# Attention and gated expert in one kernel: later chunks' output products with high and low parts side by side, first outputs in float32, and four weight tiles' low parts formed on TensorE

## The chip, the cores and the metric

The kernel runs on one core of a Trainium2 chip. The metric is the device time of one execution in microseconds (us), taken as the median of repeated runs; a shorter time is better.

## The reference

The first half is a gated recurrence per batch and head (4 batches, 8 heads, 768 steps, head dimension 48); the second is an RMS norm and a gated expert over the 3072 tokens of width 384, with a hidden width of 1536.

```
for t in range(S):
    state = alpha[:, :, t, :, None] * state + np.einsum('bhd,bhe->bhde', k[:, :, t], v[:, :, t])
    y[:, :, t] = np.einsum('bhd,bhde->bhe', q[:, :, t], state)
...
rms = np.sqrt(np.mean(x * x, axis=-1, keepdims=True) + 1e-06)
xn = x / rms * rms_g
g = xn @ w_gate
silu = g * (1.0 / (1.0 + np.exp(-g)))
val = xn @ w_val
return (silu * val @ w_out).astype(np.float32)
```

All inputs and outputs are float32; the weights reach the kernel as 64-bit words from which it takes float32.

## The kernel before

**Numbers in two parts.** Nearly every matmul operand is split in a high and a low float16 part: ScalarE (ACT) rounds to the high part, VectorE (DVE) subtracts it from the float32 value and rounds the rest to the low part. A product of two such operands is the sum of three float16 products, high by high, high by low and low by high (`SPLIT = ((0, 0), (0, 1), (1, 0))`, line 29).

**Attention.** The sequence is cut in 24 chunks of 128 tokens (`attention(cc, due)`); chunk cc belongs to batch cc mod 4, so chunks 0 to 3 are the first of their batches. For one chunk two scans of `alpha` (L549), products with k and q (L564, L569), and their low parts (L576, L603) come from DVE. Scores (`scores`, L639; in float32 for the first four chunks, L647) go to PSUM buffers with the tag `at`, of which there are three. DVE multiplies them by the mask (L652), ACT rounds to the high part (L663), DVE forms the low part (L666, `a_lo`, called `al` in the plan). `output` (L670) then makes the chunk's output `y`, 128 tokens by 8 heads of 48 columns, from two kinds of products: state by query (L680, 48 rows of weights, not for the first four chunks) and scores by v (L689, 128 rows of weights). For each of the four pairs of heads and each half j of a pair there are three products of either kind, 48 columns wide. `y` has one PSUM buffer of two banks (tag `y`, `y=1` in `BUFS`). From it ACT takes the sum of squares (L738), DVE multiplies by the RMS gain (L758); after a root on GpSimd (L754) the rows are scaled and split into `x16` (L762, L765) and transposed by a DMA into `xT` (L776). `sums` (L706) makes the state's update.

**Weights.** Eighteen tiles (`decode`): for each, ACT folds the exponent (L485), DVE does three integer steps (L494, L497, L502), ACT writes the high part (L452) and DVE the low part (L510, `wl` in the plan). Tiles i0 to i11 hold `w_gate` and `w_val`, o0 to o5 `w_out`.

**Expert.** Chunks are taken in groups of 4, 2, 2, 4, 4, 4 and 4. For each group and each of twelve blocks f of the hidden width, `expert_in` makes gate and value (L877), ACT takes silu (L888), DVE the product (L894, "gate" below), ACT and DVE its two parts (L452, L907); `expert_out` multiplies by `w_out` (L934), DVE scales the sums (L945) and a DMA stores them. In group 0 the blocks f = 0 to 2 are done in halves: first chunks 0 and 1, then 2 and 3.

**Order.** All this is entered in a `Plan` with an engine, a cost, dependences, buffers and due times. `Plan.order` (L91) walks through it once and fixes a static order for every engine; each engine then works through its own list in that order. A changed cost or operation can so move instructions all over the program.

Of the kernel before, what the change touches and what calls it, by code (L numbers as in the profile page):

```python
# [44 lines left out]
EARLY = 3  # L45

BUFS = dict(
# [8 lines left out]
    abs=0.92, wh=0.83, pow=0.65, sc=0.8, sc32=2.3, y=0.87, y0=0.5, u=0.45, po=1.48,  # L56
)
IN_COST = {4: (1.95, 0.49, 0.6, 0.63), 2: (0.99, 0.28, 0.34, 0.4)}
# [8 lines left out]
STRIDE = [0, 8, 12, 12, 20, 20, 20]  # L67


class Plan:  # L70
# [9 lines left out]
    def op(self, engine, cost, fn, deps=(), use=(), due=None, lock=False, kb=0):  # L80

        o = dict(e=engine, c=cost, fn=fn, d=[d for d in deps if d], u=tuple(use), due=due, lock=lock,
                 kb=kb, i=len(self.ops), n=[])
# [7 lines left out]
    def order(self):  # L91
        for o in reversed(self.ops):
            lat = WAIT.get(o["e"], LOAD_LAG + LOAD_END + 1.5)
            due = [n["s"] - lat for n in o["n"]] + ([o["due"]] if o["due"] is not None else [])
            o["s"] = min(due, default=1e6) - o["c"]
        free = {t: [(0.0, i) for i in range(n)] for t, n in BUFS.items()}
# [218 lines left out]
def tile_attn_moe(  # L315
# [97 lines left out]
    mask = const.tile([P, 2, 1, C], F32, name="mask")  # L413
    eps = const.tile([P, 1], F32, name="eps")
    rare = const.tile([P, 1], F32, name="rare")
    for h, rows in enumerate((slice(HC, P), slice(0, HC))):
        a0 = S_A[1] / (S_K[h] * S_Q[1])
        nc.gpsimd.memset(mask[rows, 0], a0)
        nc.gpsimd.memset(mask[rows, 1], a0 * S_QP)
    nc.gpsimd.affine_select(  # L420
        mask,
        mask,
        pattern=[[0, 2], [0, 1], [1, C]],
# [4 lines left out]
    )  # L428
    for h, rows in enumerate((slice(0, HC), slice(HC, P))):
# [7 lines left out]
    NH = len(GROUPS) * NF + EARLY  # L437
# [25 lines left out]
    def add(engine, kind, *args, **kw):  # L463
        return op(engine, COST[kind], *args, **kw)

    def decode(src, dst, name, col):
# [44 lines left out]

        raw, wu = ("raw", name), ("wu", name)
        o = op("SP", 0.9, load, [], [raw], kb=786)
# [3 lines left out]
        o = add("DVE", "rest", rest, [o], [raw, wu], lock=True)  # L517
        o = add("ACT", "wh", high, [o], [wu])
# [9 lines left out]
    def attention(cc, due):  # L528
# [129 lines left out]

        def a_tile():
# [76 lines left out]

        def square():
            nc.scalar.activation(  # L738
                like(junk), t["y"][:, :, :HW], AF.Square, accum_out=ssq[:, cc : cc + 1]
            )  # L740
# [15 lines left out]
        def gain():  # L756
            t["x32"] = tl(ap, [P, DM], F32, "x32")
            nc.vector.tensor_tensor(like(t["x32"]), t["y"][:, :, :HW], like(rg), op=ALU.mult)  # L758
# [55 lines left out]
        m0 = add("DVE", "mask", lambda: masked(0), [sc], [at0])  # L814
        m1 = add("DVE", "mask", lambda: masked(1), [sc], [at1])
        a0 = add("ACT", "a16", lambda: a_hi(0), [m0], [at0, key("a16")])
        a1 = add("ACT", "a16", lambda: a_hi(1), [m1], [at1, key("a16")])
# [363 lines left out]
```

## Time and profile before

| | |
|---|---|
| median of 3 runs | 570.16 us (568.27, 570.16, 570.45) |
| the profiled execution | 569.0 us, of which its span 567.0 us |
| TensorE (PE) busy | 513.2 us, 91% of the span |
| VectorE (DVE) busy | 411.5 us, 73% |
| ScalarE (ACT) busy | 239.0 us, 42% |

The span runs from the first to the last instruction on the core, and 2.0 us lie around it. Times in the trace count from the start of the span. Matmuls overlap each other, so that the mean length of one matmul is more than its share of the engine's time; what one costs is read from when the next begins.

### The profile page before, as it was taken

Reading aid. Unit: us, or ns where it says so; the run is one execution under the profiler, and the core shown is the slowest. Engines: PE = TensorE matmul, PEld = TensorE weight load, DVE = VectorE, ACT = ScalarE, POOL = GpSimd, SP = SyncE. Lnnn points to the kernel's source line nnn. Section 1 sums busy time; section 2 is a strip of 40 time slices with the busy share of each in tenths; the row PEclk is TensorE's granted clock in tenths of the full one; section 3 lists DMA queues with packets and bytes.
Section 4 is the critical chain, followed back from the end, with each engine's and each line's share of the span. In section 5 each row is a group of like instructions: output and inputs, shape, how many; then the busy total and the mean of one; then the engine's idle time right before and its main releaser. Section 6 shows DMA issues by size and latency. Waiting matters only on the chain.

```text
span 567.0 us, 12116 instructions
## 1 busy us (share of the span) xinstructions
PE 513.2 (91%) x4994; PEld 299.3 (53%) x4994; DVE 411.5 (73%) x739; ACT 239.0 (42%) x640; POOL 18.9 (3%) x47
## 2 busy tenths in 40 slices
PE   2445998697899899999999999999999999999995
PEld 1434643254686678644456644456545456544462
DVE  7999899999998799967877678775377643133303
ACT  2555666544444476244452245452255531133300
POOL 1100000000000000000000010000000000000000
PEclk9998899898999999999999999999999999999999
DMA  8994345567640773342334235232211101000001
GB/s 213 308 286 116 117 163 181 181 194 192 167 132 16 150 161 89 100 112 45 80 97 85 88 105 105 32 88 73 71 30 18 15 15 45 28 1 0 1 29 34
DMA packets 59695, 56.15 MB, mean 99 GB/s; under 512 B 39472, under 2 KB 54960, under 8 KB 57168
## 3 DMA queue, kind: packets, MB, share of 16 engines
q1 hardware_dynamic: 59632, 55.30, 37.6%
q8 instruction: 41, 0.67, 0.5%
q14 instruction: 22, 0.18, 0.1%
HBM read 41.26 MB, written 4.72 MB: 81 GB/s over the span
## 4 chain that ended last, share of the span: by engine, by line
PE 74%; DVE 11%; issue 1%; DMA 1%; ACT 1%; ACTq 0%
PE mm L877 41%; PE mm_po L934 22%; PE y L689 4%; PE at L639 2%; PE y L680 2%; PE at L706 1%; DVE h L907 1%; DVE h L894 1%; DVE wu_i L497 1%; DVE wu_o L502 1%; DVE wg L510 1%; DVE wu_o L497 1%; DVE wu_i L502 1%; DVE at L652 1%; DMA kT<-k 1%
## 5 line engine op out<-in xcount | busy, mean ns | idle before, releaser
L877 PE MATMUL mm<-xT,wg 128*128 128x512 f16 (+1 forms) x1566 | 292.8, 346 | 9.8 <-ACT wg L452 5.5
L877 PEld LDWEIGHTS <-wg 128*128 128x128 f16 x1566 | 151.9, 99 | 136.3 <-ACT wg L452 7.1
L934 PE MATMUL mm_po<-wo,h 128*128 128x384 f16 x864 | 149.9, 332 | 7.5 <-DVE wo L510 3.9
L934 PEld LDWEIGHTS <-h 128*128 128x128 f16 x864 | 84.2, 99 | 66.3 <-issue 14.2
L452 ACT ACTIVATE h<-h 128x512 f16<-128x512 f32 (+1 forms) x87 | 48.1, 553 | 83.6 <-DVE h L894 83.4
L894 DVE SCALAR_TENSOR_TENSOR h<-mm,sl 128x512 f32<-128x512 f32 (+1 forms) x87 | 51.7, 594 | 42.0 <-PE mm L877 42.0
L907 DVE TENSOR_TENSOR h<-h,h 128x512 f16<-128x512 f32 (+1 forms) x87 | 51.3, 591 | 20.1 <-ACT h L452 20.0
L888 ACT ACTIVATE sl<-mm 128x512 f32<-128x512 f32 (+1 forms) x87 | 45.1, 518 | 46.7 <-PE mm L877 46.1
L549 DVE TENSOR_TENSOR_SCAN att<-att,seed 112x520 f32<-112x520 f32 x48 | 59.2, 1236 | 5.3 <-DMA att<-att 4.9
L945 DVE TENSOR_SCALAR ob<-mm_po 128x384 f32<-128x384 f32 x24 | 13.2, 553 | 34.6 <-PE mm_po L934 34.6
L663 ACT CAST a<-at 128x512 f16<-128x512 f32 x48 | 28.0, 585 | 23.5 <-DVE at L652 23.3
L652 DVE TENSOR_TENSOR at<-at,mask 128x512 f32<-128x512 f32 x48 | 31.2, 693 | 5.1 <-PE at L639 4.9
L666 DVE TENSOR_TENSOR a<-at,a 128x512 f16<-128x512 f32 x48 | 30.9, 683 | 0.4
L689 PE MATMUL y<-v,a 128*128 128x48 f16 x576 | 30.4, 190 | 0.0
L647 PE MATMUL at<-qp,kh 48*128 48x128 f32 x64 | 10.4, 443 | 21.1 <-DVE qp L569 15.9
L754 POOL TENSOR_TENSOR ss<-ss,mhalf 128x1 f32<-128x1 f32 x24 | 15.7, 655 | 379.9 <-DVE ss L744 361.2
L738 ACT ACTIVATE junk<-y 128x384 bf16<-128x384 f32 x24 | 11.8, 492 | 28.0 <-DVE x L758 14.1
L689 PEld LDWEIGHTS <-a 128*128 128x128 f16 x576 | 21.3, 100 | 3.9 <-issue 0.7
L452 ACT ACTIVATE v<-v 128x384 f16<-128x384 f32 x24 | 12.5, 520 | 25.2 <-PE at L706 25.2
L576 DVE TENSOR_TENSOR k<-kh,k 112x512 f16<-112x512 f32 x24 | 16.5, 689 | 8.8 <-ACT k L452 8.7
L452 ACT ACTIVATE k<-kh 112x512 f16<-112x512 f32 x24 | 15.0, 625 | 18.4 <-DMA kT<-k 9.3
L758 DVE TENSOR_TENSOR x<-y,rg 128x384 f32<-128x384 f32 x24 | 13.3, 553 | 11.7 <-PE y L689 8.4
(86 smaller groups left out, 391.5 us busy)
## 6 DMA issues: line engine op xcount, KB each, us to landing
att<-att SPq DMA_DIRECT2D x22, 903.0 KB, 5.6
v<-vtok SPq DMA_DIRECT2D x24, 192.0 KB, 3.1
raw_i<-w_gate SPq DMA_DIRECT2D x12, 384.0 KB, 3.3
raw_i<-w_val SPq DMA_DIRECT2D x12, 384.0 KB, 4.0
raw_o<-w_out SPq DMA_DIRECT2D x6, 768.0 KB, 4.4
out_dram<-ob SPq DMA_DIRECT2D x24, 192.0 KB, 2.1
att<-att SPq DMA_DIRECT2D x4, 227.5 KB, 3.8
att<-att SPq DMA_DIRECT2D x2, 448.0 KB, 7.6
```

The costliest lines, as they stand in the source:

```text
L452: nc.scalar.activation(dst, src, AF.Copy, scale=scale, accum_out=stat[:rows, col : col + 1])
L549: nc.vector.tensor_tensor_scan(x, x, start.rearrange("r g p c -> r (g p c)"), 0.0, op0=ALU.mult, op1=ALU.add)
L576: nc.vector.tensor_tensor(t["k16"][:, 1], t["kh"], t["k16"][:, 0], op=ALU.subtract)
L652: nc.vector.tensor_tensor(t["sc"][j], t["sc"][j], mask[:, int(first)].to_broadcast([P, NP, C]), op=ALU.mult,)
L663: nc.scalar.copy(a_tile()[:, j, 0], t["sc"][j])
L666: nc.vector.tensor_tensor(a_tile()[:, j, 1], t["sc"][j], a_tile()[:, j, 0], op=ALU.subtract)
L689: nc.tensor.matmul(yps[:, j, cs], a_tile()[:, j, x, p, :], t["v16"][:, y, j, p, :], start=first and m == 0, stop=m == 2,)
L877: nc.tensor.matmul(ps[:, :n], wg[:, f, x, j, kk, :], xT[:, y, kk, cs], start=i == 0, stop=i == 3 * NK - 1,)
L888: nc.scalar.activation(t["sl"][:, :n], t[0][:, :n], AF.Silu, scale=1.0 / (S_X * S_W))
L894: nc.vector.scalar_tensor_tensor(t["h"][:, :n], t[1][:, :n], S_H / (S_X * S_W), t["sl"][:, :n], op0=ALU.mult, op1=ALU.mult,)
L907: nc.vector.tensor_tensor(h16_of(g, f)[:, 1, cs], t["h"][:, :n], h16_of(g, f)[:, 0, cs], op=ALU.subtract)
L934: nc.tensor.matmul(t[i][:, :DM], h16_of(g, f)[:, x, ts], wo[:, f // 2, y, f % 2, :], start=f == 0 and m == 0, stop=f == NF - 1 and m == 2,)
```

## The change

1. **Wide outputs.** For chunks 10 to 23 (`WIDE`), the high part of the weights is multiplied with both parts of the other operand at once, 96 columns wide, and the low part with the high part alone, 48 columns wide. A pair of heads then takes 8 products instead of 12. The results stand in two columns of sums in PSUM; ACT copies one of them to `x32` (`take`), DVE adds the other (`add_up`), and the sum of squares and the gain read `x32` in place of PSUM.
2. **First outputs in float32.** For chunks 0 to 3 (`OUT32`) the mask is multiplied straight into a float32 tile in the place of `a16`, and eight float32 products by the unsplit v give `y`. The rounding (L663) and the low part (L666) are dropped for them.
3. **Four low parts by TensorE.** For weight tiles i0 to i3 (`LOW_W`), TensorE multiplies the float32 tile by an identity into the `y` buffer, then adds minus the high part; ACT writes the rest as the low part. DVE's L510 is dropped for them.
4. **Constants** for this (a third mask, an identity in float32 and its negative in float16) are made by GpSimd at the start. Other new names (`LATE`, `LOW_A`, `LOW_H`, `CUTS`, `SIDE`, more costs) leave the plan as it was with the values given: `LOW_A` and `LOW_H` are empty.

```diff
+OUT32 = 4
+WIDE = range(10, 24)
+LOW_A = ()
+LOW_H = ()
+LOW_W = ("i0", "i1", "i2", "i3")
...
+        def bring():
+            t["ps"] = buf(ps_y, [P, 2, 512], F32, "y", name)
+            for n in range(2):
+                nc.tensor.matmul(
+                    t["ps"][:, n, : NW // 2], same, t["uf"][:, n * (NW // 2) : (n + 1) * (NW // 2)],
+                    start=True, stop=False,
+                )
+
+        def less():
+            for n in range(2):
+                nc.tensor.matmul(
+                    t["ps"][:, n, : NW // 2], minus, dst[:, 0, n * (NW // 2) : (n + 1) * (NW // 2)],
+                    start=False, stop=True,
+                )
+
+        def residue():
+            nc.scalar.copy(
+                dst[:, 1].rearrange("p (n c) -> p n c", n=2), t["ps"][:, :, : NW // 2]
+            )
...
+        if name in LOW_W:
+            ps = ("y", name)
+            o0 = add("PE", "wid", bring, [o], [wu, ps])
+            o = add("ACT", "wh", high, [o], [wu])
+            o = add("PE", "wneg", less, [o, o0], [ps])
+            return add("ACT", "wl2", residue, [o], [ps])
...
+            nc.vector.tensor_tensor(
+                tile_of(("a16", cc), make)[:, j],
+                t["sc"][j],
+                mask[:, 2].to_broadcast([P, NP, C]),
+                op=ALU.mult,
+            )
...
+                    nc.tensor.matmul(
+                        t["y"][:, j, p * D : (p + 1) * D],
+                        tiles["a16", cc][:, j, p, :],
+                        v[:, j, p, :],
+                        start=True,
+                        stop=True,
+                    )
...
+        def output_wide(h):
+            if h == 0:
+                t["y"] = tl(ps_y, [P, 2, 512], F32, "y")
+            for p in (2 * h, 2 * h + 1):
+                at = [t["y"][:, j, 2 * p * D : 2 * (p + 1) * D] for j in range(2)]
+                for x in range(2):
+                    for j in range(2):
+                        r = slice(64 * j, 64 * j + D)
+                        nc.tensor.matmul(
+                            at[j][:, : (2 - x) * D],
+                            t["q16"][r, x, p, :],
+                            states[b][2][r, : 2 - x, p, :],
+                            start=x == 0,
+                            stop=False,
+                        )
+                for j in range(2):
+                    for x in range(2):
+                        nc.tensor.matmul(
+                            at[j][:, : (2 - x) * D],
+                            a_tile()[:, j, x, p, :],
+                            t["v16"][:, : 2 - x, j, p, :],
+                            start=False,
+                            stop=x == 1,
+                        )
...
+            nc.scalar.copy(t["ys4"], y_part(1))
...
+            nc.vector.tensor_tensor(t["ys4"], y_part(0), t["ys4"], op=ALU.add)
...
+        if cc < OUT32:
+            m0 = add("DVE", "mask", lambda: masked32(0), [sc], [at0, key("a16")])
+            m1 = add("DVE", "mask", lambda: masked32(1), [sc], [at1, key("a16")])
+            ins = [key("a16"), key("v"), key("y")]
+            y0 = add("PE", "y32", lambda: output32(0), [m0, m1, lv], ins)
+            y1 = add("PE", "y32", lambda: output32(1), [y0], ins)
...
+        if cc in WIDE:
+            y_k = key("x32")
+            y1 = add("ACT", "take", take, [y1], [key("y"), y_k])
+            y1 = add("DVE", "add", add_up, [y1], [key("y"), y_k])
+        sq = add("ACT", "sq", square, [y1], [y_k])
+        x = add("DVE", "x", gain, [sq if cc in WIDE else y1, tiles["rg"]], [y_k, key("x32")], lock=cc in WIDE)
```

**VectorE around the first gate of the expert** (`h32_0_0_0`, chunks 0 and 1, f = 0), before: the last chunk of group 0 and the scans of chunk 4 stand ahead of it (`att`, `qp`, `x16`: the number behind is the chunk's; L549 is a scan).

```order
L765 SCALAR_TENSOR_TENSOR x16_2_529<-x32_2_457,ss_2_455,x16_2_529 128x384
L549 SCALAR_TENSOR_TENSOR att_4_178<-att_4_178,seed_91 112x520
L744 TENSOR_SCALAR ss_3_547<-ssq_115,eps_98 128x1
L758 TENSOR_TENSOR x32_3_549<-y_3_511,rg_90 128x384
...
L549 SCALAR_TENSOR_TENSOR att_4_178<-att_4_178,seed2_95 112x520
L765 SCALAR_TENSOR_TENSOR x16_3_566<-x32_3_549,ss_3_547,x16_3_566 128x384
L894 SCALAR_TENSOR_TENSOR h32_0_0_0_591<-mm_0_0_0_1_568,sl_0_0_0_578 128x256
```

The same place now (L602 is a scan, L898 the low part of x, L1046 the gate; `wu_i3` is the fourth weight tile).

```order
L602 SCALAR_TENSOR_TENSOR att_5_233<-att_5_233,seed2_95 112x520
L622 TENSOR_TENSOR qp_5_468<-att_5_233 112x2x4x64
L656 SCALAR_TENSOR_TENSOR q16_4_451<-qp_4_398,q16_4_451 112x512
...
L529 SCALAR_TENSOR_TENSOR wu_i3_512<-raw_i3_297,wu_i3_512 128x768
L891 TENSOR_TENSOR x32_3_532<-y_3_490,rg_90 128x384
...
L602 SCALAR_TENSOR_TENSOR att_6_383<-att_6_383,seed_91 112x520
L898 SCALAR_TENSOR_TENSOR x16_3_551<-x32_3_532,ss_3_525,x16_3_551 128x384
L1046 SCALAR_TENSOR_TENSOR h32_0_0_0_571<-mm_0_0_0_1_554,sl_0_0_0_564 128x256
```

Scans of chunks 5 and 6, query products of chunks 4 and 5 and the integer steps of tiles i2 and i3 have moved ahead of the first gate, which is VectorE's instruction 81 now and was 71.

**TensorE at the first outputs**, before: the output of chunk 0 is 24 float16 products between the float32 scores of chunks 1 and 2 (`y_0`, `at_1`, `at_2`).

```order
L647 MATMUL at_1_1_198<-qp_1_174,kh_1_170 128x128
L689 LDWEIGHTS a16_0_185
L689 MATMUL y_0_212<-v16_0_189,a16_0_185 128x48
...
L647 MATMUL at_2_0_255<-qp_2_247,kh_2_225 128x128
L647 MATMUL at_2_1_256<-qp_2_247,kh_2_225 128x128
```

Now (`x8` and `x2`: so many float32 products alike; `y_i0` is the weight tile i0 in the `y` buffer).

```order
L700 MATMUL at_1_1_199<-qp_1_186,kh_1_182 128x128
L732 MATMUL y_0_214<-v_0_145,a16_0_193 128x48 x8
L700 MATMUL at_2_0_237<-qp_2_230,kh_2_228 128x128
...
L700 MATMUL at_2_1_238<-qp_2_230,kh_2_228 128x128
L732 MATMUL y_1_257<-v_1_147,a16_1_221 128x48 x8
L542 MATMUL y_i0_292<-wu_i0_235,same_109 128x384 x2
L549 LDWEIGHTS minus_107
L549 MATMUL y_i0_292<-wg_130,minus_107 128x384
```

The buffer `y` is now used in the order y_0, y_1, i0, i1, y_2, y_3, i2, i3, and the first product of the expert stands behind y_3, as before.

**TensorE in an output of a later chunk**, before: the end of the six state products of a pair, and the first of its six products of scores by v (chunk 12).

```order
L680 LDWEIGHTS q16_12_3144
L680 MATMUL y_12_3589<-s160_375,q16_12_3144 128x48
L689 LDWEIGHTS a16_12_3571
L689 MATMUL y_12_3589<-v16_12_3484,a16_12_3571 128x48
L689 LDWEIGHTS a16_12_3571
```

Now, the last three of a pair's four state products and the first two of its four products by v.

```order
L748 MATMUL y_12_3498<-s160_367,q16_12_3079 128x96
L748 LDWEIGHTS q16_12_3079
L748 MATMUL y_12_3498<-s160_367,q16_12_3079 128x48
...
L757 LDWEIGHTS a16_12_3481
L757 MATMUL y_12_3498<-v16_12_3391,a16_12_3481 128x96
L757 LDWEIGHTS a16_12_3481
L757 MATMUL y_12_3498<-v16_12_3391,a16_12_3481 128x48
```

A chunk has 32 products instead of 48, half of them 96 columns wide.

## Rows read from the trace of the kernel before

**Rows 1.** The page: span, and each engine's busy time, share and instructions.

```profile
span 567.0 us, 12116 instructions
PE 513.2 (91%) x4994; PEld 299.3 (53%) x4994; DVE 411.5 (73%) x739; ACT 239.0 (42%) x640; POOL 18.9 (3%) x47
```

**Rows 2.** Stretches: start:end, length, busy us of each engine, PEclk (TensorE's granted clock).

```profile
0.00:42.80 42.80, 16.64 (x257) 14.36 (x258) 38.17 (x62) 18.86 (x49) 4.42 (x21) 1.00 1.01 270
42.80:55.20 12.40, 6.52 (x43) 4.49 (x39) 12.29 (x21) 6.86 (x22) 0.55 (x1) 0.93 0.33 84
55.20:132.10 76.90, 65.88 (x395) 34.23 (x396) 74.06 (x109) 44.53 (x114) 0.72 (x5) 0.92 0.55 170
132.10:150.50 18.40, 15.95 (x246) 10.12 (x246) 17.30 (x36) 7.20 (x18) 1.10 (x2) 0.91 0.63 164
150.50:196.20 45.70, 44.07 (x625) 34.41 (x625) 40.80 (x85) 20.89 (x69) 1.41 (x2) 1.00 0.48 116
196.20:474.90 278.70, 278.05 (x2991) 157.88 (x2984) 203.79 (x382) 123.23 (x330) 10.12 (x15) 1.00 0.32 73
```

**Rows 3.** Chain that ended last, 129 to 198: start, us, what.

```profile
131.20 0.87 DVE wo L510
...
143.65 2.93 PE mm_po L934 x18
...
149.28 0.61 DVE a L666
...
150.49 22.70 PE mm L877 x207
```

**Rows 4.** TensorE's timeline, 268 to 300: start, us, operation, shapes, count.

```profile
290.62 0.84 PE L639 MATMUL at<-q,k 48*128 48x128 f16 x24
291.40 4.06 PE L877 MATMUL mm<-xT,wg 128*128 128x512 f16 x18
295.39 0.24 PE L680 MATMUL y<-s,q 48*128 48x48 f16 x6
295.57 0.32 PE L689 MATMUL y<-v,a 128*128 128x48 f16 x6
295.82 0.25 PE L680 MATMUL y<-s,q 48*128 48x48 f16 x6
...
297.04 3.25 PE L934 MATMUL mm_po<-wo,h 128*128 128x384 f16 x19
```

**Rows 5.** Groups by line and shape: count, then busy us, mean ns of one, idle before.

```profile
L549 DVE TENSOR_TENSOR_SCAN att<-att,seed 112x520 f32<-112x520 f32 x48 | 59.2, 1236 | 5.3 <-DMA att<-att 4.9
L666 DVE TENSOR_TENSOR a<-at,a 128x512 f16<-128x512 f32 x48 | 30.9, 683 | 0.4
L758 DVE TENSOR_TENSOR x<-y,rg 128x384 f32<-128x384 f32 x24 | 13.3, 553 | 11.7 <-PE y L689 8.4 <-ACT junk L738 3.2
L738 ACT ACTIVATE junk<-y 128x384 bf16<-128x384 f32 x24 | 11.8, 492 | 28.0 <-DVE x L758 14.1 <-PE y L689 13.6
L497 DVE SCALAR_TENSOR_TENSOR wu_i<-raw_i,wu_i 128x768 int32<-128x768 int32 x12 | 11.5, 958 | 0.4
L510 DVE TENSOR_TENSOR wg<-wu_i,wg 128x768 f16<-128x768 f32 x12 | 11.4, 949 | 0.0
```

**Rows 6.** Timeline of the first outputs, 0 to 45, TensorE's rows.

```profile
17.24 2.04 PE L647 MATMUL at<-qp,kh 48*128 48x128 f32 x14 [3.46 <-DVE a L666]
...
19.21 1.20 PE L689 MATMUL y<-v,a 128*128 128x48 f16 x24
...
24.88 1.14 PE L689 MATMUL y<-v,a 128*128 128x48 f16 x24
...
25.95 0.25 PE L706 MATMUL at<-v,kT 64*64 64x48 f16 x1
```

**Rows 7.** Timeline behind one output, 293 to 303: squares, then the transposing DMA.

```profile
297.23 0.49 ACT L738 ACTIVATE junk<-y 128x384 bf16<-128x384 f32 x1 [0.22 <-PE y L689]
...
300.36 1.22 SPq L776 DMA_TRANSPOSE xT<-x  x1
```

More of the change, by code (lines that the diff above doesn't have):

```diff
@@ L95, in order @@
             o["s"] = min(due, default=1e6) - o["c"]
+        for o in self.ops:
+            o["s"] += o["late"]
         free = {t: [(0.0, i) for i in range(n)] for t, n in BUFS.items()}
@@ L411, in tile_attn_moe @@
     nc.gpsimd.memset(seed2, 0.0)
-    mask = const.tile([P, 2, 1, C], F32, name="mask")
+    mask = const.tile([P, 3, 1, C], F32, name="mask")
     eps = const.tile([P, 1], F32, name="eps")
@@ L419, in tile_attn_moe @@
         nc.gpsimd.memset(mask[rows, 1], a0 * S_QP)
+        nc.gpsimd.memset(mask[rows, 2], a0 * S_QP * S_V)
     nc.gpsimd.affine_select(
@@ L428, in tile_attn_moe @@
     )
+    minus = const.tile([P, P], F16, name="minus")
+    nc.gpsimd.memset(minus, 0.0)
+    same = const.tile([P, P], F32, name="same")
+    nc.gpsimd.memset(same, 0.0)
+    for x, value in ((minus, -1.0), (same, 1.0)):
+        nc.gpsimd.affine_select(
+            x, x, pattern=[[1, P]], compare_op=ALU.not_equal, fill=value, base=0,
+            channel_multiplier=-1,
+        )
     for h, rows in enumerate((slice(0, HC), slice(HC, P))):
@@ L463, in add @@
     def add(engine, kind, *args, **kw):
-        return op(engine, COST[kind], *args, **kw)
+        return op(engine, COST[kind], *args, late=LATE.get(kind, 0.0), **kw)
     def decode(src, dst, name, col):
@@ new lines, in y_part, with take, add_up, a_less @@
+        def y_part(x):
+            y = t["y"][:, :, : 2 * HW].rearrange("s j (p x e) -> s j p x e", p=NP, x=2)
+            return y[:, :, :, x]
+        def take():
+            t["x32"] = tl(ap, [P, DM], F32, "x32")
+            t["ys4"] = t["x32"].rearrange("s (j p e) -> s j p e", j=2, p=NP)
+            nc.scalar.copy(t["ys4"], y_part(1))
+            t["ys"] = like(t["x32"])
+        def add_up():
+            nc.vector.tensor_tensor(t["ys4"], y_part(0), t["ys4"], op=ALU.add)
+        def a_less(j):
+            nc.tensor.matmul(
+                t["sc"][j].rearrange("s p c -> s (p c)"),
+                minus,
+                a_tile()[:, j, 0].rearrange("s p c -> s (p c)"),
+                start=False,
+                stop=True,
+            )
@@ L659, in a_tile, with a_rest @@
+        def a_rest(j):
+            nc.scalar.copy(a_tile()[:, j, 1], t["sc"][j])
         def a_tile():
@@ L813, in attention @@
             sc = add("PE", "sc", scores, [kl, ql], [key("k16"), key("q16"), at0, at1])
[L814 to L817, printed above, removed]
-        l0 = add("DVE", "al", lambda: a_lo(0), [a0], [at0, key("a16")])
-        l1 = add("DVE", "al", lambda: a_lo(1), [a1], [at1, key("a16")])
@@ L909, in h_lo, with h_less, h_rest @@
             )
+        def h_less():
+            nc.tensor.matmul(t["h"][:, :n], minus, h16_of(g, f)[:, 0, cs], start=False, stop=True)
+        def h_rest():
+            nc.scalar.copy(h16_of(g, f)[:, 1, cs], t["h"][:, :n])
+        low_pe = g in LOW_H
         end = now + 2 * step * PACE[g]
@@ L964, in expert_out @@
             now += step
-            tail[0] = op("PE", COST["po"], part, [tail[0]] + deps, use, due=now)
+            tail[0] = op("PE", cost, part, [tail[0]] + deps, use, due=now)
         for i in range(n):
@@ L1013, in tile_attn_moe @@
             now = expert_in(g, f, c0, c1, now, deps)
-        side = [3, 1] if g == 0 else [1] * m
+        side = SIDE if g == 0 else [1] * m
         t0 = 0
```

90 lines of the change are left out of this document (65 added, 25 removed).

## The prediction

> **What bounds the kernel now.** I read the page first: TensorE is busy 91% of the span, VectorE 73%, ScalarE 42%, GpSimd 3% [rows 1]. Such averages hide stages, so I cut the span where the work changes hands [rows 2]. Up to 42.8 us VectorE is busy 38.2 us and TensorE 16.6, and from 55.2 to 132.1 VectorE 74.1 of 76.9: the first quarter belongs to VectorE. From 196.2 to 474.9 TensorE is busy 278.05 of 278.70 us: there the end is TensorE's work alone, and everything that it does less comes off. The chain shows the handover: VectorE's last low part of `w_out` at 131.20, one more VectorE piece at 149.28, and from 150.49 the products of group 1 in one run [rows 3]. So I ask two things: how much TensorE work goes after about 196 us, and how much earlier VectorE lets TensorE get there.
>
> **Wide outputs (chunks 10 to 23).** In the timeline a pair of heads is a block of six state products from 295.39 to 295.57 (0.18 us, 30 ns each) and a block of six by v from 295.57 to 295.82 (0.25 us, 42 ns each) [rows 4]: 0.43 us for twelve. There are 14 chunks of four pairs, 56 pairs. If a product costs the same at 96 columns as at 48, eight instead of twelve save a third, 0.145 us a pair and 8.1 us in all. That is the upper bound. For the lower, each of the four wide products pays its 48 added columns in full. The rate is in the row of 512-column products: 18 of them from 291.40 to 295.39, 0.222 us each, 0.43 ns a column, so 21 ns more for a wide one, 83 ns a pair. Then 0.062 us a pair and 3.5 us are left. Between them decides the nearest row: 24 products of the same 48-row weights, but 128 columns wide, run from 290.62 to 291.40, 32.5 ns each [rows 4]. So 80 more columns cost a state product 2.5 ns. For the products by v no such row exists, but 96 columns at 0.43 ns are 41 ns, just under their present spacing. I take 4 ns for a wide one, 16 ns a pair, 0.9 us: **7.2 us saved**.
>
> Here a rule speaks against the change. TensorEngine Tiling (Array Packing) in the Trainium skill, "Instruction Overhead", says that each matmul has an overhead of about 60 cycles, so that one column takes as long as 60. By it a 48-column product would cost 25 ns at 2.4 GHz and a 96-column one 40, a pair 260 instead of 300 ns, and the 56 pairs would save an estimated 2.2 us. The trace does not agree: products of 48 columns stand 30 and 42 ns apart, and of 128 columns 32.5.
>
> The price is a copy on ACT and an addition on VectorE for each of these chunks. The nearest rows are 0.49 us (squares from the same PSUM tile) and 0.55 us (gain from it) [rows 5], so 6.9 and 7.7 us in all. They lie in a stretch where ACT idles 155 of 279 us and VectorE 75 [rows 2], and I cost them at nothing. What could be late is the chunk's `xT`: from the start of the squares to its DMA's issue are 3.1 us now [rows 7], to which come 0.49 and 0.55 and two handovers of 0.2 (the squares start 0.19 us after the output's end, 297.04 [rows 4, 7]), about 1.5. In the new order the last output before group 3 is followed by 63 products by `w_out` at 0.163 us (18 take 2.93 [rows 3]), 10.3 us, before group 3 begins. The cover is double the 4.6 us and a landing. If it were gone, each of the groups 3 to 6 would begin about 1.5 us late, 6 us together.
>
> **Less VectorE work in the first quarter.** Dropped are eight low parts of scores at 30.9/48 = 0.64 us and four of weights at 0.95 [rows 5]: 5.2 and 3.8, together 9.0 us. The mask multiplications remain. Counting VectorE's list, the first gate of group 2 is its instruction 307 and was 319; ahead of it stand the same instructions but for these twelve. If VectorE set the pace up to there, all 9.0 us would show. If none of it reached TensorE, nothing would.
>
> The lists show why it should be less. Ahead of the very first gate VectorE's work grows: three scans more (1.24 each), six integer steps of weights, six products or low parts of 0.64 to 0.69, and small ones, 14.3 us, against 8.5 us dropped there, so 5.8 us more. Ahead of the last low part of `w_out` it is still 4.0 us more, because chunks 4 to 6 are further on. VectorE hardly idles before this point [rows 2], so I move its end from 132.07 to 136.1. What TensorE has left there is less than before: 18 products by `w_out` (2.9 us); chunk 6's output, which waits for five VectorE instructions of about 0.64 (3.4 us with a handover, the later of the two); that output itself (295.39 to 297.04, 1.65 us); and 36 products (5.9). Group 1 then begins at 136.1 + 3.4 + 1.65 + 5.9 = 147.0 instead of 150.49, 3.5 us earlier. From there to group 2 TensorE works almost without a break (44.1 of 45.7 us [rows 2]): chunk 6's output is no longer in that stretch (1.65 us), and since VectorE's lead grows, I give half of the 1.6 us of idle time (0.8). **6.0 us** in all, between 0 and 9.0.
>
> **Float32 products on TensorE.** The first outputs cost more there. Of the float32 scores 14 records (seven products of 128 columns, two halves side by side) start at 17.24, and the next work at 19.21: 0.14 us a record, two records a product, so eight products take 2.3 us, and up to 4.5 if the side-by-side halves of the present ones hide half. The 24 float16 products took 1.07 us (24.88 to 25.95) [rows 6]. That is 1.2 to 3.4 us more a chunk. A weight tile takes two float32 products of 384 columns, three times the 0.28 us of one of 128, 1.7 us and up to 3.4, and two float16 ones of 0.163. In all 13 to 28 us more TensorE work, nearly all before 55.2 us, where TensorE idles 26.2 and 5.9 us [rows 2]. I cost it at nothing; the cover is that idle time, and once it is used up each further microsecond goes on to the first gate. On the other side, the score buffers come free a rounding and a low part earlier: TensorE sat idle 3.46 us before 17.24 for one [rows 6]. ACT loses eight roundings and gains four copies. GpSimd makes its constants while it idles.
>
> **The sum.** 569.0 - 7.2 - 6.0 = 555.8 us for the profiled execution (567.0 of span and 2.0 around it). The median of the runs shown stands 1.2 us above that execution; I add it and predict **557.0 us**.
>
> **Rivals.**
> - *The whole lead comes through.* VectorE sets the pace up to group 2; 9.0 + 7.2 give 554. For it: VectorE is busy 74.1 of 76.9 us. Against: TensorE has hardly any idle time from 150.49 on that could be given back. 0.17.
> - *The lead is eaten at the start.* The first gates are 6 us later, and the stretch behind, where TensorE is busy 65.9 of 76.9 us [rows 2], can't make that up; only the 7.2 remain: 563. For it: the 5.8 us of added work ahead of the first gate. 0.19.
> - *Columns cost in full.* The wide products pay 0.43 ns for each column: 3.5 + 6.0 give 560.7. For it: 512-column products do pay this. Against: the 128-column row. 0.09. The rule of the Trainium skill's TensorEngine Tiling (Array Packing), section "Instruction Overhead", would end near here, at an estimated 562.
> - *The single `y` buffer becomes the bound: slower.* It now passes from y_0 through i0, i1, y_2, y_3 to i2, one after the other, and the third block of the expert waits for i2. With float32 products at their upper prices, 4.5 and 3.4 us, and 0.75 to 1.8 us for reading and handing on, four outputs (21 us) and three tiles (15.5) from 17.2 us end at 54, just when that block begins now (55.2). Should TensorE fall to its lower granted clock (1.2 GHz) here, where it idles much, its parts double, some 29 us more: even with 13 us given back elsewhere, 586. It decides once that chain ends after about 68 us, where the 13 us gained elsewhere are used up. Against: the granted clock was 1.00 up to 42.8 [rows 2]. 0.08.
> - *No change.* The wide products save 3.5 us, and that much is lost where `xT` comes late: 570. 0.04.
>
> **The numbers.** The forecast, both terms between their inner bounds, has 0.43. Less than 0.5% (2.9 us) can't be told from no change with such runs. All cases but the last two end faster by more, 0.88; I keep some for mixtures of the third with losses at the start: faster 0.85, same 0.07, slower 0.08. The range goes from both upper bounds, 569.0 - 8.1 - 9.0 + 1.2 = 553, with 1 us for buffers that come free earlier, to the lower one of the wide products alone, 569.0 - 3.5 + 1.2 = 566.7: 552 to 566, which leaves out the last two cases and little else.
>
> **What would show it.** Wide: a pair's block shrinks from 0.43 to about 0.31 us, and the stretch between the group starts with it. Early: the first gate of the expert comes at about 52 us instead of 47, the last low part of `w_out` ends near 136, group 1 begins near 147, group 2 near 190. Float32: eight products take 2.3 to 4.5 us. The prediction is wrong if the third block of the expert starts after 60 us, if TensorE shows idle time at the starts of groups 3 to 6, or if a pair's block stays above 0.37 us.

## The result: 5 us faster, where 13 were forecast

The changed kernel took 563.93 us (median of 4 runs, 563.83 to 564.21), the kernel before 569.21 in the same comparison (568.26 to 570.45): ratio 0.991, 95% interval [0.988, 0.993]. Its profiled execution took 563.84 us with a span of 561.7, 5.3 us less than the span before. The page's head, as in [rows 1]:

```profile
span 561.7 us, 11676 instructions
PE 523.1 (93%) x4762; PEld 306.2 (55%) x4762; DVE 408.4 (73%) x741; ACT 243.7 (43%) x650; POOL 24.5 (4%) x53
```

TensorE has 232 records less and is nevertheless busy 10 us longer: the work added at the start (busy 105.4 us up to 132.1, 89.0 before) is larger than what the wide outputs took off. The stretches of [rows 2], in the same cuts:

```profile
0.00:42.80 42.80, 24.64 (x220) 19.57 (x220) 38.13 (x61) 17.02 (x46) 6.04 (x26) 0.97 0.98 269
42.80:55.20 12.40, 10.63 (x59) 8.61 (x60) 12.18 (x25) 7.74 (x24) 1.86 (x2) 0.71 0.77 166
55.20:132.10 76.90, 70.10 (x595) 38.51 (x593) 75.79 (x119) 48.61 (x126) 2.07 (x7) 0.96 0.62 181
...
196.20:474.90 278.70, 274.38 (x2650) 150.78 (x2648) 202.25 (x378) 123.54 (x322) 12.57 (x15) 0.99 0.29 69
```

In the last of them TensorE was busy 278.05 us before and is busy 274.38 now: 4.3 us of idle time stand in a stretch that had 0.65. Where it sits is found by setting the starts of the groups against each other. In the kernel before, TensorE's timeline has these rows at the starts of groups 2, 3 and 4, the last with the state update ahead of it:

```profile
196.19 1.05 PE L877 MATMUL mm<-xT,wg 128*128 128x256 f16 x8
240.65 1.03 PE L877 MATMUL mm<-xT,wg 128*128 128x512 f16 x4
323.74 0.56 PE L706 MATMUL at<-v,kT 64*64 64x48 f16 x48
324.23 1.04 PE L877 MATMUL mm<-xT,wg 128*128 128x512 f16 x4
```

and in the changed kernel these, for groups 1, 2 and 3, the output half of group 3 (286.39; 297.04 before, [rows 4]) and group 4:

```profile
144.13 23.74 PE L1029 MATMUL mm<-xT,wg 128*128 128x256 f16 x216
186.62 3.12 PE L1029 MATMUL mm<-xT,wg 128*128 128x256 f16 x27
230.99 1.25 PE L1029 MATMUL mm<-xT,wg 128*128 128x512 f16 x5
286.39 0.81 PE L1099 MATMUL mm_po<-wo,h 128*128 128x384 f16 x4
319.21 4.02 PE L1029 MATMUL mm<-xT,wg 128*128 128x512 f16 x9
```

Group 1 comes 6.4 us earlier, group 2 9.6, group 3 9.7, its output half 10.65. Then group 4 comes only 5.0 us earlier, and about so it stays to the end. By stretches the 5.3 us are -9.6 up to group 2, -1.1 from there to 286.39, +5.6 from there to 319.21 and -0.3 behind it. The third is a new wait. TensorE's rows there:

```profile
313.00 0.59 PE L837 MATMUL at<-v,kT 64*64 64x48 f16 x49
314.51 0.54 PE L837 MATMUL at<-v,kT 64*64 64x48 f16 x47 [0.92 <-DVE st L855]
318.44 0.83 PE L837 MATMUL at<-v,kT 64*64 64x48 f16 x48 [3.40 <-DMA kT<-k]
319.21 4.02 PE L1029 MATMUL mm<-xT,wg 128*128 128x512 f16 x9
```

L837 is `sums`, the update of a chunk's state. The plan now lets those of chunks 12, 13 and 14 follow each other ahead of group 4; before, only that of chunk 12 stood there (323.74), and the others in the fifth block of group 4 and behind its ninth. There are two `kT` buffers, so the third update's transposed keys can be fetched only once the first has released its own. The chain of work that ended last shows this fetch on the path:

```profile
313.07 0.57 PE at L837 x39
313.64 0.02 issue
313.66 4.74 DMA kT<-k
318.40 0.04 issue
318.44 0.83 PE at L837 x34
```

After this idling the first nine products of group 4 take 4.02 us where nine take 2.0 otherwise; the granted clock of the stretch is 0.50, the 1.2 GHz level:

```profile
319.20:323.20 4.00, 4.00 (x15) 1.23 (x13) 2.80 (x7) 0.62 (x2) 0.00 (x0) 0.50 1.11 198
```

The trace's record of the clock has 0.50 from 316.35, inside the second idle time, to 323.18, and 1.00 from there. So the 5.6 us up to group 4 are 0.9 and 3.4 us of idle time, 1.0 for the two updates moved ahead of it (half a microsecond each, which group 4 then saves) and 0.3 for the third one's slower run; behind the start of group 4 come another 2.0 us for its first nine products.

The wide outputs themselves, which were to save 7.2 us, show one pair after the other like this (four of eight rows):

```profile
264.24 0.24 PE L748 MATMUL y<-s,q 48*128 48x96 f16 x4
264.41 0.31 PE L757 MATMUL y<-v,a 128*128 128x96 f16 x4
264.65 0.24 PE L748 MATMUL y<-s,q 48*128 48x96 f16 x4
264.82 0.31 PE L757 MATMUL y<-v,a 128*128 128x96 f16 x4
```

A pair is 0.17 us of state products and 0.24 of products by `v`: 0.41 instead of 0.43 [rows 4], with eight products instead of twelve. The starts of the single records of TensorE, which these rows sum up, tell why. In the kernel before, products by `v` stand 25 ns apart (38 behind the first of a block). State products start in twos, one of either half, 3 to 4 ns apart, and from two to two there are 21 to 36 ns. Wherever a product with 48-row weights follows one with 128-row weights, or the other way, the next starts 111 to 116 ns after. In the changed kernel the products by `v` stand 28 to 54 ns apart, the wider ones at the upper end, the twos of state products 50, and the gaps at the changes are 111 to 117 ns.

The loading of the next weights is late there as well: among products by `v` it begins 1 to 11 ns behind a product, but the first load for `v` at 295.567 comes 108 ns behind the last state product (295.459). It is the number of rows that matters. From the last product by `v` to the first by `w_out`, both with 128 rows, there are 25 ns (297.013 to 297.038). And the surcharge is there with other products as well: a product of 512 columns is followed by one of 128 rows after 216 ns and by one of 48 rows after 311, one of 384 columns after 163 and 258. Nor is it a wait for the sums: from `v` to the next pair's state products, which begin new sums, the gap is as long as inside a pair, where the products add to the same ones. A pair has two changes, 0.23 of its 0.43 us from start to start; of each some 0.09 us go beyond a product's own 25 ns, so that about 0.18 us of a pair never belonged to the products. The Trainium skill has the matching rule in TensorEngine Tiling (Array Packing), section "Key Properties": changing the tiling mode drains the TensorE. It gives no price; the trace's is 111 to 117 ns from start to start. What TensorE does in the gap no run here shows.

### The profile page after: what moved, and what is told of

Its sections match the earlier page's. It is cut to its first block, busy times and chain, and to the rows that moved or that the text cites. A ratio compares the mean times of both kernels' runs of the same rounds, so it can differ in the third digit from the quotient of the medians.

```text
span 561.7 us, 11676 instructions
## 1 busy us (share of the span) xinstructions
PE 523.1 (93%) x4762; PEld 306.2 (55%) x4762; DVE 408.4 (73%) x741; ACT 243.7 (43%) x650; POOL 24.5 (4%) x53
## 4 chain that ended last, share of the span: by engine, by line
PE 80%; DVE 14%; issue 2%; ACT 2%; DMA 1%; DVEq 0%; ACTq 0%
PE mm L1029 47%; PE mm_po L1099 24%; DVE att L602 3%; PE y L757 2%; PE at L692 2%; PE y L748 2%; PE at L837 1%; DVE wu_i L524 1%; DMA kT<-k 1%; PE y L820 1%; DVE a L719 1%; DVE h L1046 1%; DVE h L1059 1%; DVE x L891 1%; DVE wu_i L521 1%
## 5 line engine op out<-in xcount | busy, mean ns | idle before, releaser
L1046 DVE SCALAR_TENSOR_TENSOR h<-mm,sl 128x512 f32<-128x512 f32 (+1 forms) x87 | 51.5, 592 | 42.5 <-PE mm L1029 41.8
L602 DVE TENSOR_TENSOR_SCAN att<-att,seed 112x520 f32<-112x520 f32 x48 | 59.2, 1235 | 3.2 <-DMA att<-att 2.6
L886 POOL TENSOR_TENSOR ss<-ss,mhalf 128x1 f32<-128x1 f32 x24 | 20.2, 842 | 447.4 <-DVE ss L876 430.3
L1110 DVE TENSOR_SCALAR ob<-mm_po 128x384 f32<-128x384 f32 x24 | 13.2, 553 | 33.8 <-PE mm_po L1099 33.7
L794 ACT CAST a<-at 128x512 f16<-128x512 f32 x40 | 23.1, 583 | 20.8 <-DVE at L705 20.5
L705 DVE TENSOR_TENSOR at<-at,mask 128x512 f32<-128x512 f32 x40 | 26.1, 691 | 8.1 <-PE at L692 8.0
L797 DVE TENSOR_TENSOR a<-at,a 128x512 f16<-128x512 f32 x40 | 26.0, 682 | 0.6 <-ACT a L794 0.2
L895 ACT ACTIVATE x<-x,ss 128x384 f16<-128x384 f32 x24 | 14.6, 610 | 14.6 <-POOL ss L886 13.6
L700 PE MATMUL at<-qp,kh 48*128 48x128 f32 x64 | 8.2, 401 | 11.4 <-DVE qp L622 10.6
L837 PE MATMUL at<-v,kT 64*48 64x48 f16 (+1 forms) x960 | 12.2, 190 | 5.7 <-DMA kT<-k 3.4
L692 PEld LDWEIGHTS <-k 48*128 48x128 f16 x480 | 13.4, 94 | 7.5 <-issue 6.3
L757 PE MATMUL y<-v,a 128*128 128x96 f16 x224 | 17.2, 197 | 0.0
```

What stands on the lines that cost most here:

```text
L602: nc.vector.tensor_tensor_scan(x, x, start.rearrange("r g p c -> r (g p c)"), 0.0, op0=ALU.mult, op1=ALU.add)
L692: nc.tensor.matmul(o, t["k16"][r, x, p, :], t["q16"][r, y, p, :], start=m == 0, stop=m == 2,)
L705: nc.vector.tensor_tensor(t["sc"][j], t["sc"][j], mask[:, int(first)].to_broadcast([P, NP, C]), op=ALU.mult,)
L757: nc.tensor.matmul(at[j][:, : (2 - x) * D], a_tile()[:, j, x, p, :], t["v16"][:, : 2 - x, j, p, :], start=False, stop=x == 1,)
L794: nc.scalar.copy(a_tile()[:, j, 0], t["sc"][j])
L797: nc.vector.tensor_tensor(a_tile()[:, j, 1], t["sc"][j], a_tile()[:, j, 0], op=ALU.subtract)
```

## The experiments

The theory A that these runs test has two halves: a change between the two kinds of weights costs about 0.09 us whatever the number and width of the products, and the run of three updates ahead of group 4 costs 5.6 us. All ratios are to the kernel before, run beside each of these kernels on the same chip; its median was 570.5 to 571.9 there.

| kernel | us | ratio, 95% interval |
|---|---|---|
| wide_fewer | 558.81 | 0.978 [0.975, 0.981] |
| wide_more | 578.64 | 1.014 [1.011, 1.017] |
| no_wide | 560.01 | 0.980 [0.978, 0.983] |
| before_fewer | 566.06 | 0.991 [0.988, 0.994] |
| after_spread | 558.18 | 0.977 [0.974, 0.981] |
| wide_only | 575.34 | 1.008 [1.005, 1.011] |
| nowide_fewer | 553.32 | 0.969 [0.965, 0.972] |
| fewer_spread | 552.64 | 0.968 [0.964, 0.971] |
| f32_only | 566.78 | 0.993 [0.991, 0.995] |
| loww_only | 570.56 | 1.001 [0.998, 1.003] |
| all_fewer_spread | 551.28 | 0.966 [0.963, 0.968] |

**Fewer changes, same products (wide_fewer).** The core of the edit in `output_wide`, with the two loops as functions `from_state` and `from_v`:

```diff
-            for p in (2 * h, 2 * h + 1):
-                ...   # state products of p, then products by v of p
+            p, q = 2 * h, 2 * h + 1
+            from_v(p, False)
+            from_state(p, True)
+            from_state(q, False)
+            from_v(q, True)
```

> The changed kernel, with one edit: in the wide outputs of chunks 10 to 23, the two pairs of a half go in the order v products, state products, state products, v products, instead of state, v, state, v. Same products, same columns, same order of everything else; the changes between products with 48-row weights and products with 128-row weights fall from 8 to 4 in a chunk, 56 less in all. Theory A (the gap of some 112 ns at each such change, against 25 to 50 ns between products of one kind, is what the eight products did not remove): 56 times about 0.09 us, 5.0 us less than the changed kernel, about 559 us. Rival B (the time of a block goes by its products and their columns): no difference, 563.9 us, within 1 us.

Measured: 0.978 against the changed kernel's 0.991, some 7 us less; by spans 556.5 against 561.7, 5.2 us. One chunk's output in TensorE's timeline:

```profile
304.51 0.29 PE L759 MATMUL y<-v,a 128*128 128x96 f16 x4
304.74 0.31 PE L748 MATMUL y<-s,q 48*128 48x96 f16 x8
304.98 0.44 PE L759 MATMUL y<-v,a 128*128 128x96 f16 x8
305.35 0.31 PE L748 MATMUL y<-s,q 48*128 48x96 f16 x8
305.59 0.30 PE L759 MATMUL y<-v,a 128*128 128x96 f16 x4
305.74 6.01 PE L1107 MATMUL mm_po<-wo,h 128*128 128x384 f16 x36
```

From the first row to the last there are 1.23 us for the same 32 products that took 1.55 in the changed kernel (264.24 to 265.79). Four products by `v` and the change take 0.23 us, eight and the change 0.37: four more cost 0.14 us, 35 ns each, and where one pair's products meet the next pair's of the same kind no gap is seen. The run of three updates stands here as in the changed kernel, with 0.92 and 3.33 us of idle time ahead of group 4, so the difference is not due to it. Theory A holds, B doesn't.

**More changes, same products (wide_more).**

```diff
-                for x in range(2):
-                    for j in range(2):
-                        r = slice(64 * j, 64 * j + D)
+                for j in range(2):
+                    r = slice(64 * j, 64 * j + D)
+                    for x in range(2):
                         ...   # state product
-                for j in range(2):
                     for x in range(2):
                         ...   # product by v
```

> The changed kernel, with one edit: in each pair of the wide outputs, state products of half 0, v products of half 0, state products of half 1, v products of half 1. Same products and columns; the changes between the two kinds double, 112 more in all, and the two halves' state products no longer lie side by side. Theory A (each change costs a gap of about 0.09 us): about 10 us more than the changed kernel, 574 us; up to 2.8 us more where the state products no longer overlap (56 pairs by 0.05). Rival B (products and columns): at most these 2.8 us, 564 to 567 us.

Measured: 578.64 us, 1.014, 13 us above the changed kernel by the ratios, 14 by the spans. The same chunk's output now runs from 310.79 to the products of `w_out` at 313.42, 2.63 us, in rows of two products:

```profile
310.79 0.24 PE L748 MATMUL y<-s,q 48*128 48x96 f16 x2
310.95 0.24 PE L756 MATMUL y<-v,a 128*128 128x96 f16 x2
311.13 0.24 PE L748 MATMUL y<-s,q 48*128 48x96 f16 x2
311.29 0.24 PE L756 MATMUL y<-v,a 128*128 128x96 f16 x2
...
313.42 6.01 PE L1098 MATMUL mm_po<-wo,h 128*128 128x384 f16 x36
```

From 4 to 7 to 15 changes inside a chunk's output, 1.23, 1.55 and 2.63 us: 0.11 and 0.13 us a change. The second is a little dear since the two halves' state products no longer lie side by side.

**The early parts without the wide outputs (no_wide).**

```diff
-WIDE = range(10, 24)
+WIDE = range(0)
```

> The changed kernel without the wide outputs: chunks 10 to 23 as in the kernel before, twelve products a pair; the first outputs in float32 and the four weight tiles' low parts by TensorE stay. Its order has the state updates of groups 3 and 4 spread as before. Theory A (the lead of 9.6 us at group 3 is lost where the order of the wide kernel lets state updates of three chunks follow each other ahead of group 4): the lead comes through, 569.2 - 9.6 = 559.6 us, faster than the changed kernel. Rival B (the lead is given back in any case when group 4 waits for its own attention): 569.2 - 5.0 = 564 us or, without the 1.2 us that the wide products saved, 565 us. Rival C (the wide products themselves gained the 5 us and the early part nothing that lasts): 568 to 570 us.

Measured: 560.01 us, 0.980, faster than the changed kernel. One update stands ahead of group 4 (314.44), without idle time. Group 2 begins at 186.94 and group 4 at 314.93, 9.3 us ahead of the kernel before at both: the lead comes through. So the wide outputs, meant to save 7 us, made this kernel slower than it would have been without them.

**The kernel before with fewer changes (before_fewer)**, the same edit as wide_fewer in `output` of the kernel before.

> The kernel before, with one edit: in the outputs of chunks 4 to 23 the two pairs of a half go in the order v, state, state, v. Same twelve products a pair; 80 changes between 48-row and 128-row weights less. Theory A (0.09 us a change): 80 times 0.09, 7.2 us less, about 562 us, more than the whole of the wide products' eight-for-twelve saved (1.2 us). Rival B (products and columns): 569.2 us, within 1 us.

Measured: 0.991, 5 us: less than the 7.2 worked out, but as much as the whole change gained, without one product less. In its profiled execution the time from the start of group 2 (199.06) to the last output half (531.96) is 332.9 us, against 339.8 in the kernel before (196.19 to 536.02): 6.9 us for the 60 changes less in chunks 9 to 23, 0.115 us each; 0.09 us each would be 5.4, and where the rest comes from is open. But group 2 began 2.9 us later than before. A part of it is the clock: its record has 0.50 from 150.15 to 153.57, where group 1 starts (151.22), and 1.00 there in the kernel before. The rest was not followed up.

**The same instructions, updates spread (after_spread).** `yw` is the cost that the planner assumes for a half of a wide output.

```diff
-y=0.87, y0=0.5, y32=1.85, yw=0.6,
+y=0.87, y0=0.5, y32=1.85, yw=0.87,
```

> The changed kernel, with one number of the planner's table of costs set otherwise: yw 0.87 instead of 0.6, which alters no instruction but lets the plan spread the state updates of chunks 12, 13 and 14 as in the kernel before (one ahead of group 4, one in its fifth, one in its eighth block of the input half), instead of all three in a row ahead of group 4. Theory A (the run of three updates costs some 5.6 us: 0.9 us and 3.4 us of idle TensorE and some 2 us at half the granted clock, less what the spread ones cost): 558 to 559 us, 0.981 of the kernel before, and no idle time of more than 1 us ahead of group 4. Rival B (the lead is lost to something that the wide outputs themselves bring, wherever the updates stand): 564 us, with another wait in the stretch.

Measured: 558.18 us, 0.977. TensorE's rows at the start of group 4:

```profile
310.72 3.25 PE L1099 MATMUL mm_po<-wo,h 128*128 128x384 f16 x19
313.90 0.56 PE L837 MATMUL at<-v,kT 64*64 64x48 f16 x48
314.46 5.99 PE L1029 MATMUL mm<-xT,wg 128*128 128x512 f16 x27
```

One update, no idle time, and 27 products in 5.99 us instead of 9 in 4.02. From the output half of group 3 (287.29) to group 4 are 27.2 us, as in the kernel before (297.04 to 324.23), against 32.8 in the changed kernel. The wait comes with the order and goes with it, as theory A has it.

**The wide outputs alone (wide_only).**

```diff
-OUT32 = 4
+OUT32 = 0
-LOW_W = ("i0", "i1", "i2", "i3")
+LOW_W = ()
```

> The kernel before with the wide outputs alone: first outputs in float32 and the weight tiles' low parts by TensorE taken back. Its order has the three state updates in a row ahead of group 4 again. Theory A (the wide products save 1.2 us and the run of updates costs 5.6 us): 4 us slower than the kernel before, ratio 1.008. Rival B (the run costs only what an early lead has to give back, and this kernel has none): 1 us faster than before to no change. Rival C (the wide products gain what was forecast): 5 to 7 us faster.

Measured: 575.34 us, slower, 1.008. The run of updates is there again, without any lead, with a shorter wait for `kT` and a further one for `xT`:

```profile
328.43 0.59 PE L837 MATMUL at<-v,kT 64*64 64x48 f16 x49
329.94 0.54 PE L837 MATMUL at<-v,kT 64*64 64x48 f16 x47 [0.92 <-DVE st L855]
332.38 0.56 PE L837 MATMUL at<-v,kT 64*64 64x48 f16 x48 [1.90 <-DMA kT<-k]
333.68 2.74 PE L1029 MATMUL mm<-xT,wg 128*128 128x512 f16 x6 [0.74 <-DMA xT<-x]
```

The ratio is theory A's, but not by the run of updates alone. In the profiled execution, 3.7 us longer than the median of its runs, group 2 already begins 5.0 us later than in the kernel before, behind another wait for `xT`, which theory A doesn't have:

```profile
201.15 4.46 PE L1029 MATMUL mm<-xT,wg 128*128 128x256 f16 x27 [1.87 <-DMA xT<-x]
```

How much of this the other executions share is not shown, so this run can't price the run of updates; after_spread does.

**Both causes mended (nowide_fewer, fewer_spread, all_fewer_spread).** No new code: the order v, state, state, v with `WIDE` empty, in the wide outputs with `yw` at 0.87, and in all outputs with `yw` at 0.87.

> The changed kernel without the wide outputs (twelve products a pair in all chunks), with the order v, state, state, v of the two pairs of a half in chunks 4 to 23: 80 changes between the two kinds of weights less. If the price of a change seen in the other runs holds (5 us for these 80), and early parts and outputs add up: 0.980 - 0.009 = 0.971 of the kernel before, 553 us.

> The changed kernel with both edits: wide outputs of chunks 10 to 23 in the order v, state, state, v, and yw 0.87, which spreads the state updates of chunks 12 to 14. If the two causes are separate and add up: 0.978 (the first alone) less 0.010 (the run of updates) = 0.968 of the kernel before, 551 us. If they are one cause, no more than either alone, 0.978.

> The changed kernel with the order v, state, state, v in all outputs of chunks 4 to 23, wide or not, and yw 0.87: 24 changes between the two kinds of weights less than with that order in the wide outputs alone. At the price of a change that the other runs show (5 us for 56 to 80 of them): 1.5 to 2 us less than that kernel's 552.6 us, 0.965 of the kernel before, 551 us. Rival (these chunks' outputs lie under other waits of the early part): no difference.

Measured: 553.32, 552.64 and 551.28 us, each within 2 us of its expectation: the two causes add up. The last is the fastest of all, 0.966 of the kernel before. Against nowide_fewer, which differs from it only in the wide products and their copy and addition, it gains 0.3% by the ratios (their intervals overlap), 2.0 us by the medians and 3.4 by the spans (552.9 and 549.5), where the profiled execution of nowide_fewer was the longest of its six. So where changes are few, eight wide products instead of twelve look worth some 2 us, hardly clear of the noise.

**The two early parts singly (f32_only, loww_only)**, with `WIDE` empty and either `LOW_W` empty or `OUT32` at 0.

> The kernel before with the first outputs in float32 alone (no wide outputs, no low parts of weights by TensorE). It takes 8 low parts of 0.64 us from VectorE's early queue. Theory A (the early gain is VectorE's time ahead of the first gates, and the parts add up): 8 times 0.64 = 5.1 us of the 9 us that the two early parts take away, some 5 us faster than the kernel before, ratio 0.991. Rival B (the early gain needs both, since either alone leaves the same transfer or the other half of the queue as the bound): less than 2 us faster.

> The kernel before with the low parts of the weight tiles i0 to i3 by TensorE alone. It takes 4 operations of 0.95 us from VectorE's early queue and puts 16 float32 and half-precision products on TensorE. Theory A (the parts add up): 4 times 0.95 = 3.8 us faster, ratio 0.993. Rival B (either alone leaves the bound): less than 1.5 us faster.

Measured: 0.993, 4 us, and 1.001, nothing; together (no_wide) they give 0.980, 11 us. Singly the first is near theory A's 5 us and the second is rival B's; but added up they give 4 us and not 11, and on the adding up theory A was wrong. With the weights alone, group 1 begins at 142.8, 7.6 us early, but then the attention of chunks 7 to 9 stands in a row ahead of group 2, which begins at 197.51 (196.19 before):

```profile
185.27 0.56 PE L837 MATMUL at<-v,kT 64*64 64x48 f16 x47 [2.36 <-DVE a L797]
188.70 1.44 PE L692 MATMUL at<-q,k 48*128 48x128 f16 x23 [0.82 <-DVE st L855]
193.01 0.83 PE L837 MATMUL at<-v,kT 64*64 64x48 f16 x47 [2.70 <-DVE a L797]
197.51 2.74 PE L1029 MATMUL mm<-xT,wg 128*128 128x256 f16 x12
```

The clock adds to it: its record has 0.50 from 187.17 to 200.83. With the first outputs alone the last low part of `w_out` ends a little earlier than before, at 131.43, but group 1 begins at 150.29, as before. A wait for VectorE's attention and the output of chunk 6 stand ahead of it:

```profile
147.28 0.56 PE L837 MATMUL at<-v,kT 64*64 64x48 f16 x47 [2.54 <-DVE a L797]
```

The profile of f32_only shows only 1.0 us less span than that of the kernel before, its timed runs 4 us. Its profiled execution lies 1.0 us above the median of its runs, and that of the kernel before 1.2 us below the median of the runs shown with it, which is most of the difference; what follows goes by the timed runs.

## Why the prediction was wrong

The direction was right and 563.9 us lies in the range, but the gain was 5.3 us for 13.2, by two steps that failed and one that was too cautious. That the time still lies in the range is luck: the early gain, larger than forecast, made up for part of the other two. Of the signs that were to show the prediction wrong, two came: idle time at the start of group 4, and a pair's block above 0.37 us (0.41).

- **Wide outputs, -7.2 forecast, -1 to -2 measured** (a chunk's output takes 1.55 instead of 1.65 us, 1.3 for 14 chunks; after_spread stands 0.3%, 1.7 us, under no_wide, with intervals that overlap)**.** The failed step is "If a product costs the same at 96 columns as at 48, eight instead of twelve save a third". It shared out a pair's 0.43 us evenly over twelve products. The block also held two changes between kinds of weights, some 0.18 us of it beyond the products' own time, and these stayed. What was left of it for the products gave less than a third, since wider ones do cost more: by `v`, products of 48 columns stand 25 ns apart and of 96 columns 42. The 128-column row that decided between the bounds is one of 24 products of one kind, with no change in it and two halves side by side, and was set against an average that was half gaps. Both bounds, 3.5 and 8.1, were missed, since both shared out the whole block. The rule that was set aside here was nearest. By "Instruction Overhead" in the Trainium skill's TensorEngine Tiling (Array Packing) the 60 cycles are an estimated 25 ns at 2.4 GHz and 96 columns 40 ns, and the products by `v` agree, with 25 and 42. The state products don't one by one, as they start in twos, and so the estimated 2.2 us were still more than the 1.3 measured. The trace seemed to speak against the rule only while the gaps of 111 to 116 ns were averaged into the spacing (0.25 us for six, 42 ns each).
- **The order behind group 3, 0 forecast, +5.6 measured.** "TensorE's work alone, and everything that it does less comes off" took the late stretch as fixed. The prediction looked at the order around the outputs and at `xT`, not at the state updates that the plan moved. That TensorE "shows idle time at the starts of groups 3 to 6" was named as a sign that the prediction is wrong, and so it does, at group 4; the wait is for `kT`, not for `xT`, which had cover enough in the changed kernel.
- **Early VectorE work, -6.0 forecast, -9.6 measured.** This step is right in kind and mis-sized: the whole lead comes through, as the first rival had it. The last low part of `w_out` ends at 133.73 and not 136.1 (before: 132.07), group 1 begins at 144.1 and not 147.0, group 2 at 186.6 and not near 190. Of the 3.6 us, 2.4 are the first of these. The term behind it moved that end by all of the 4.0 us of added work since "VectorE hardly idles before this point"; but up to 132.1 VectorE idled 7.6 us before and idles 6.0 now (the first three stretches), so idle time took up 1.6 of them. Of the rest, 0.5 come between there and group 1 and 0.8 up to group 2. VectorE's rows:

```profile
53.48 0.41 DVE L1046 SCALAR_TENSOR_TENSOR h<-mm,sl 128x256 f32<-128x256 f32 x1
132.78 0.95 DVE L537 TENSOR_TENSOR wo<-wu_o,wo 128x768 f16<-128x768 f32 x1
```

 The first gate, forecast at about 52, was at 53.5, so the start was indeed later and was made up. That the 9.6 us lie near the 9.0 of the removed work doesn't show that they are this work: its two parts don't add up (f32_only, loww_only).
- **Float32 products, costed at nothing, 2.3 to 4.5 us each.** Right as far as the trace shows. The chain of work that ended last does pass through the products of one weight tile (2.90 us at 27.68, 0.65 at 30.58), but VectorE is busy 4.81 of the 5.00 us from 27.6 to 32.6, so little can have been lost there; no run prices the float32 products alone. Three of the four blocks took 3.65 us and one, under the range, 1.99. The single `y` buffer did hold TensorE up once, 4.48 us ahead of 44.06, without becoming the bound: the third block of the expert, with 60 us as the limit, starts at 56.95 (55.22 before). Against that rival stood "the granted clock was 1.00 up to 42.8", and this reading was wrong. The trace's record of the granted clock has no entry ahead of 46.56 in the kernel before and ahead of 33.04 in the changed one, and the views print 1.00 where there is none. The pace there is that of the lower level: 216 ns between float32 records at 16.22 as at 44.06, where the record has 0.50, and 114 at 37.59, where it has 1.00. So the clock half of the rival's condition came true, and the chain through `y` still ended in time.

```profile
16.22 3.65 PE L732 MATMUL y<-v,a 128*128 128x48 f32 x16
...
37.59 1.99 PE L732 MATMUL y<-v,a 128*128 128x48 f32 x16
44.06 3.65 PE L732 MATMUL y<-v,a 128*128 128x48 f32 x16 [4.48 <-ACT junk L872]
...
56.95 1.92 PE L1029 MATMUL mm<-xT,wg 128*128 128x256 f16 x16 [1.46 <-ACT wg L555]
```

## What to carry to other kernels

Before a block of short products is costed by their number, look at the starts of its single records, not at an average: where weights of different row counts alternate, the gaps at the changes may be half of the block, and putting like beside like saves them without leaving out any work. Where a planner sets the order, a cheaper operation moves others; read the new order at every handover between stages, and look there for users of one buffer pool that now stand in a row. Two savings on the same path need not add up: each alone may run into what only the other removes, as the two early parts here gave 4 us singly and 11 together. Where a view gives a full clock, see whether the trace has an entry for that time, and set the pace of like instructions against it.

## What the runs showed of the hardware

- A change between products with 48-row and with 128-row weights takes 111 to 119 ns from start to start in all of these kernels, measured behind 140 us where the granted clock is 1.00. Products of one kind follow each other after 21 to 54 ns (state products in twos that start 3 to 4 ns apart). The change is nearly the same in both directions and with 48 or 96 columns, behind products of 384 and 512 columns it adds 95 ns (258 instead of 163, 311 instead of 216), and the load of the next weights begins 107 to 116 ns behind the last product of the other kind.
- TensorE's pace in the first 30 us is half of the later one: float32 records of the first outputs stand 216 ns apart at 16.22 and 21.96, 114 at 37.59, and 216 again at 44.06. The record of the granted clock begins at 33.04, with 1.00 to 39.87 and 0.50 to 50.11; ahead of it there is no entry. The other kernels agree: in f32_only the record begins at 52.16 and all four blocks have 216 ns, and in loww_only, where it begins at 43.81, the float16 products by `v` of the first outputs stand 40 ns apart up to then and 25 at 45.15. So the first stretch runs at the pace of the lower level, and the 1.00 that the views give for it is no measurement.
- In the changed kernel the record falls to 0.50 three times ahead of the end, each time inside idle time of TensorE: at 39.87 (4.48 us idle ahead of 44.06), at 111.55 (2.69 ahead of 112.49) and at 316.35 (3.40 ahead of 318.44). The 2.0 us lost so behind 319.21 add to the idle time itself.
